# Turning the first two tiles centred, v's weights on ScalarE's queue, and a new order list

## The chip, the cores and the metric

The kernel runs on one core of one Trainium2 chip. The metric is the device time of one execution in microseconds (us). Of the kernel before there are three timed runs, and one more execution that was profiled. The core has a matrix engine (TensorE, PE in the profile, its weight loads PEld), a vector engine (VectorE, DVE), an activation engine (ScalarE, ACT), GpSimd (POOL), and SyncE (SP), which here issues transfers only. Transfers go out from the queues of SP, ACT and POOL and share 16 DMA engines.

## The reference

The input x is 2048 rows of 512, in bfloat16, and every row is normalised first (mean and variance over the 512). Two branches start from that normalised row, xn:

```python
xn = layernorm(x)
q, k, v = split(xn @ wqkv)              # 32 heads of 16
s = local_attention(q, k, v) @ wo       # row i sees rows i, i-2, ..., i-14
h = gelu(layernorm(xn) @ w1)
hs = shift_rows_by_group(h) @ w2        # four column groups, rows -1, +1, -2, +2
x1 = xn + hs
b = x1 + gelu(layernorm(x1) @ w3) @ w4  # w3 is 512x1376, w4 is 1376x512
out = x + s * silu(b)                   # the outer x, not xn
```

`layernorm` has eps 1e-5 and no learned factor. What matters here is that a row's normalisation is a subtraction of its mean and a multiplication by one number per row, so the number can also be applied after a product.

## The kernel before

The 2048 rows are 16 tiles of 128 rows, four tiles to a chunk of 512, four chunks. Tile i of chunk c holds every fourth row of the chunk. One long string, `ORDER`, lists some 700 steps such as `v.0.1` (the v product of tile 0 into PSUM bank 1), and the program issues them in just that order. Each engine runs its own steps in the order in which they stand in the list, and waits by semaphores for what it needs. A transfer also waits until the transfer that held its semaphore lane eight transfers earlier has landed. So moving a step in the list moves it past everything else on its engine or queue.

The steps around the change, with the lines of the profile:

- Loading. `ldxp.s.0` loads tiles 0 and 1 as one transfer of 256 KB from SP's queue (L221), `ldv.s.0` and `ldv.s.1` v's weights in halves of 256 KB (L234), then `ldxp.s.1` tiles 2 and 3, `ldw1.s.0` and `.1` w1 in halves (L241), two more pairs of x, and the weights of q and of k (`ldqk`, L228), 512 KB each. All go out from SP.
- Warming. `c_warm` fills a tile (L275) and `warmup` runs products on it that nobody reads (L321), ten of 512 columns before the first real work and eight of 128 columns inside it.
- Statistics. `st.i` takes a tile's mean and variance on DVE (L333 and L334). For tiles 0 to 3, `sq0.i` is the square root on ACT (L338), and `nm0.i` the reciprocal (L344) and the normalised tile `xr[i]` (L345) on DVE. For the other tiles the factor comes from a power on POOL (`rs`, L386) and the tile from `nmv` on DVE (L410) or `nm` on ACT (L417).
- Turning. The products need xn with its 512 columns on the partitions. Tiles 0 to 3 are turned on PE, `tr0.i` (L356), four transposes each, and copied out of PSUM by ACT into `xnT` of chunk 0, `ev0h` in two halves for tiles 0 and 1 (L364), `ev0a` for 2 and 3 (L360). From tile 4 on a transposing DMA does it, one for a pair of tiles, `xT.k` on SP (L424).
- Products. `v.i` (L471), copied out by `ev.i` on ACT (L481) and stored to HBM by `sv.i` on POOL (L489); `w1.i` (L496), copied out with gelu by `eh.i` (L507), whose row factor `rs` and `rr` (L397) have made; `qk.c.n` (L443), eight products for a whole chunk, copied out by `eqk` (L452).
- Later. `hTr` and `x1Tr` are transposing DMAs on SP for h and for the normalised x1; `w2`, `w3`, `w4`, `wo` are the other products; `pw` (L530), `smx`, `sms`, `smn` and `vp` (L716) are the attention's work on DVE, `lg` (L543) and `ws` (L729) its sums on PE.
- The end. Tiles 12 to 14 go through `ge` (ACT, L782), `gb` (L786) and `fav` (L819) on DVE and leave by `so` (L839). Tile 15 is done in two halves, `woh` (PE, L793), `sgh` (L802) and `favh` (L807) on DVE, `soh` (L813).

Of the kernel before, what the change touches and what calls it, by code (L numbers as in the profile page):

```python
# [20 lines left out]
st.4 tr0.3.3 rs.1 v.2.1 ev0a.3 st.7 rp.2 rs.2 w1.2.4 ev.2 st.6 eh.0 v.3.3 sv.2 rp.3 rr.1 w1.3.1  # L21
nmv.4 nmv.5 ev.3 qk.0.1.5 xT.2 eh.1 sv.3 qk.0.0.3 rs.3 qk.0.3.2 eh.2 eh.3 eqk.0.1 c_elog
qk.0.4.1 qk.0.5.5 nmv.6 nmv.7 st.11 ldxc.s.3 st.10 st.8 eqk.0.3 eqk.0.5 qk.0.2.2 eqk.0.0
qk.0.6.4 eqk.0.2 st.9 eqk.0.4 qk.0.7.3 eqk.0.6 eqk.0.7 pw.0.1 rp.5 st.15 st.13 rp.4 xT.3 hTr.0
ldw2.s hTr.1 w1.4.1 v.5.4 ldwo.s.0 ev.5 w1.5.3 v.4.2 ev.4 qk.1.4.4 rs.4 sv.4 v.6.5 w1.7.2 rr.3
rr.2 eh.4 pw.0.2 kh.1 ev.6 sv.5 rs.5 nb.4 pw.0.0 st.12 eqk.1.4 eh.5 w1.6.1 qk.1.1.4 qk.1.2.3
v.7.5 hTr.2 nm.8 nm.9 w2.1.0 pw.0.3 nb.5 rp.6 eh.6 xT.4 vl.s.1.1 eh.7 st.14 rp.7 lg.0.0 rs.7
eqk.1.2 lg.0.1 ev.7 pw.0.5 w2.0.5 rs.6 eqk.1.1 nm.11 nm.10 pw.0.4 sv.7 qk.1.5.4 sv.6 xT.5
qk.1.6.3 xa.1 nb.7 qk.1.0.2 nb.6 st3s.1 eqk.1.6 hTr.3 rr.4 xa.0 ldw3.s.0 st3s.0 eqk.1.5 pw.0.6
nm.13 nm.12 nm.15 qk.1.7.0 qk.1.3.4 w2.2.5 w1.9.3 w1.8.1 eh.9 eh.8 xa.2 rr.7 hTr.4 rr.5 rq.0  # L30
w1.10.5 pw.0.7 r3.0 v.8.3 eh.10 st3s.2 nm.14 w2.3.1 nm3.0 nm3.1 eqk.1.3 w2.5.5 ev.8 qk.2.0.4
xa.3 st3s.3 eqk.1.7 eqk.1.0 xT.6 lg.0.3 rq.1 kh.2 xa.5 lg.0.2 r3.1 w2.4.2 smx.0 ldw3.s.1 sv.8
xT.7 x1Tr.0 v.10.5 qk.2.4.0 w2.6.1 eqk.2.4 nm3.3 xa.4 ex.0 w2.7.3 w1.11.2 xa.6 st3s.6 nm3.2 xa.7
qk.2.5.1 eqk.2.0 x1Tr.1 eh.11 ev.10 sv.10 rr.6 v.9.0 v.11.3 w1.13.4 eqk.2.5 ev.9 hTr.5 qk.2.7.2
w1.15.1 eqk.2.7 w1.12.0 vl.s.2.0 vl.s.0.0 ldw4.s.2 qk.2.2.2 vl.s.3.1 eh.12 pw.1.0 st3s.4 st3s.7
st3s.5 v.12.5 eqk.2.2 pw.1.3 sms.0 eh.13 v.13.0 w3.0.6.4 ev.11 hTr.6 rq.2 qk.2.1.3 pw.1.2 r3.2
sv.9 eg.0.6 eqk.2.1 ldwo.s.3 smn.0 rq.3 pw.1.1 r3.3 w3.0.1.2 qk.2.3.4 w3.0.10.3 nm3.4 eqk.2.3
tE.0 eh.15 eg.0.10 ev.13 eg.0.1 lg.1.1 lg.1.0 pw.1.7 w2.8.1 w1.14.0 w3.0.0.2 eh.14 w3.0.2.3
hTr.7 qk.2.6.0 eqk.2.6 eg.0.0 w2.10.4 nm3.6 vl.s.0.1 nm3.7 x1Tr.3 vl.s.1.0 pw.1.5 xa.8 pw.1.4
nm3.5 pw.1.6 w2.11.1 xa.10 w3.0.8.2 xa.11 qk.3.1.4 st3s.11 eg.0.8 ev.12 w2.14.1 lg.1.2 st3s.10  # L40
sv.12 lg.1.3 eqk.3.1 w2.12.4 sv.11 st3s.8 eg.0.2 smx.1 w2.9.3 ldw4.s.1 x1Tr.2 xa.9 w2.15.5 xa.14
w3.0.3.2 w3.0.9.3 xa.12 pw.2.2 qk.3.2.1 qk.3.0.4 w2.13.0 st3s.9 eqk.3.2 eqk.3.0 eg.0.3 vl.s.9.1
ldw4.s.0 rq.4 xa.15 vl.s.9.0 vl.s.3.0 ldwo.s.2 pre.s.2 qk.3.3.1 w3.0.5.2 st3s.12 qk.3.4.5 eg.0.5
pw.2.3 eqk.3.3 qk.3.5.4 st3s.14 pw.2.4 xa.13 pw.2.1 rq.5 st3s.15 v.15.1 eqk.3.5 v.14.2 ev.15
eqk.3.4 w3.1.1.0 w3.0.4.5 vp.0 st3s.13 rq.6 pw.2.0 r3.4 nm3.9 w3.0.7.1 eg.0.4 ev.14 eg.0.9
eg.0.7 ex.1 qk.3.7.4 w3.1.0.2 eg.1.0 sv.14 r3.5 nm3.10 rq.7 nm3.11 x1Tr.5 w3.1.8.1 vl.s.2.1
# [27 lines left out]
def kernel(  # L74
# [199 lines left out]
    def c_warm():  # L274
        nc.vector.memset(warm[:], 0.0)  # L275

    @step
    def c_ident():
        make_identity(nc, ident[:])
# [4 lines left out]
        nc.gpsimd.memset(mhalf[:], -0.5)  # L284

    @step
    def c_zero():
        nc.gpsimd.dma_start(out=v_dram[0:PADK, :], in_=warm[0:PADK, :])
        nc.gpsimd.memset(hT[:, :, :, 0:HALO], 0.0)
        nc.gpsimd.memset(hT[:, :, :, HALO + S // TPC :], 0.0)  # L290

# [51 lines left out]
    def nm0(i):
        nc.vector.reciprocal(out=rstd1(i), in_=ve1[:, i // 2, i % 2 : i % 2 + 1])  # L344
        nc.vector.tensor_scalar(  # L345
            out=xr[i], in0=xtile(i), scalar1=mv1[:, i, 0:1], scalar2=rstd1(i),
            op0=ALU.subtract, op1=ALU.mult,
        )
# [3 lines left out]
    @step  # L352
    def tr0(i, b):
        tr_t[i] = bank(b, (P, ND, P), BF16)
        for dt in range(ND):
            nc.tensor.transpose(tr_t[i][:, dt, :], xr[i][:, dt * P : (dt + 1) * P], ident[:])  # L356
# [5 lines left out]
    @step  # L362
    def ev0h(i, h):
        nc.scalar.activation(  # L364
            xnT_tile(0)[:, i, 2 * h : 2 * h + 2, :], tr_t[i][:, 2 * h : 2 * h + 2, :], AF.Copy
        )
# [98 lines left out]

    @step
    def v(i, b):
        c, jj = i // TPC, i % TPC
        pt = mm["v", i] = bank(b)
        for dt in range(ND):  # L470
            nc.tensor.matmul(  # L471
                pt, lhsT=xnT[c][:, jj, dt, :], rhs=wv_sb[:, dt, :],
                start=(dt == 0), stop=(dt == ND - 1),
            )

# [14 lines left out]

    @step
    def w1(i, b):
        c, jj = i // TPC, i % TPC
        pt = mm["w1", i] = bank(b)
        for dt in range(ND):
            nc.tensor.matmul(  # L496
                pt, lhsT=xnT[c][:, jj, dt, :], rhs=w1_sb[:, dt, :],
                start=(dt == 0), stop=(dt == ND - 1),
            )

# [374 lines left out]
```

## Time and profile before

| | |
|---|---|
| median of three timed runs | 190.42 us (190.27 to 190.52) |
| profiled execution | 190.75 us |
| its span, first to last instruction | 189.0 us |
| outside the span | 1.75 us |
| mean granted TensorE clock | 0.996 |
| busy in the span: PE, DVE, ACT, POOL | 182.8, 165.1, 112.8, 42.7 us |
| moved by DMA | 39.25 MB, 208 GB/s on average |

The rows of the profile give the start and the duration of instructions on each engine, merged where the same operation repeats ("x4"), with the idle time ahead of them in square brackets and what ended it. "Issue to landing" of a transfer runs from the issuing instruction's start until all of its data has arrived. A product of 512 columns is shown with a duration of 379 ns, but the next one starts 216 ns after it: four of them take 0.86 us in the chain of waits.

### The profile page before, as it was taken

The numbers are of one execution on the slowest core, as the hardware profiler recorded it, in microseconds if no ns is written. First come the engines' busy times: TensorE is split into PE (matmuls) and PEld (weight loads), VectorE is DVE, ScalarE is ACT, GpSimd is POOL, SyncE is SP. The second block draws the span as 40 slices with busy tenths as digits, with TensorE's granted clock in tenths as the row PEclk, the third lists the DMA queues.
The fourth block names the chain that finished last, engine by engine and source line by source line (L and its number), as shares of the span: only waits on it lengthen the run. The fifth ranks groups of instructions, "written<-read, shape, count | busy, mean of one in ns | idle before, by whom it ended". The sixth has DMA issues, their size and how long they took to land.

```text
span 189.0 us, 3685 instructions
## 1 busy us (share of the span) xinstructions
PE 182.8 (97%) x1430; PEld 87.0 (46%) x1430; DVE 165.1 (87%) x270; ACT 112.8 (60%) x189; POOL 42.7 (23%) x70
## 2 busy tenths in 40 slices
PE   7999999999999999999999999999999999999990
PEld 2444445445444545444444555444455444444450
DVE  2694797997999899999989998999999999989554
ACT  3578669666595636045941465969529664742780
POOL 4157156423010702010450000000050003005350
PEclk9999999999999999999999999999999999999998
DMA  5994986987969929965989929999974999796783
GB/s 164 315 352 115 199 248 141 194 238 137 233 120 286 278 64 224 222 87 190 399 162 361 274 57 134 254 401 277 189 190 95 254 335 238 210 254 106 88 106 116
DMA packets 47842, 39.25 MB, mean 208 GB/s; under 512 B 35251, under 2 KB 41889, under 8 KB 47777
## 3 DMA queue, kind: packets, MB, share of 16 engines
q1 hardware_dynamic: 45008, 35.14, 74.6%
q0 software_dynamic: 2528, 3.69, 10.9%
q8 instruction: 11, 0.18, 0.4%
q10 hardware_dynamic: 288, 0.20, 0.3%
q14 instruction: 7, 0.05, 0.1%
HBM read 26.41 MB, written 5.78 MB: 170 GB/s over the span
## 4 chain that ended last, share of the span: by engine, by line
PE 85%; DMA 4%; DVE 4%; issue 2%; POOL 2%; SPq 1%; ACT 1%; POOLq 0%
PE mm L668 20%; PE mm L685 18%; PE mm L443 15%; PE mm L611 8%; PE mm L496 7%; PE mm L471 6%; PE lg L543 4%; PE mm L768 4%; DMA xc<-in_A_x_dram 3%; PE mm L729 3%; POOL out_dram L835 2%; DMA out_dram<-xr 1%; DVE st L333 1%; DVE xr L775 1%; DVE xr L786 1%
## 5 line engine op out<-in xcount | busy, mean ns | idle before, releaser
L530 DVE TENSOR_TENSOR pw<-qT,kT 128x2048 bf16<-128x2048 bf16 x32 | 38.3, 1214 | 3.4 <-PE lg L543 2.4
L668 PE MATMUL mm<-x1T,w_sb 128*128 128x512 bf16 (+1 forms) x176 | 40.9, 379 | 0.0
L685 PE MATMUL mm<-w_sb,h 128*128 128x512 bf16 (+1 forms) x176 | 39.4, 379 | 0.0
L677 ACT ACTIVATE h<-mm 128x512 bf16<-128x512 f32 (+1 forms) x44 | 23.9, 602 | 23.3 <-PE mm L668 17.6
L716 DVE TENSOR_TENSOR vs<-vs,att 128x4096 bf16<-128x4096 bf16 x16 | 36.2, 2285 | 0.0
L443 PE MATMUL mm<-xnT,wqk_sb 128*128 128x512 bf16 x128 | 30.6, 379 | 0.0
L835 POOL DMA_DIRECT2D out_dram<-xr x12 | 11.0, 1117 | 74.0 <-DVE xr L775 74.0
L668 PEld LDWEIGHTS <-w_sb 128*128 128x128 bf16 (+1 forms) x176 | 17.6, 100 | 20.4
L685 PEld LDWEIGHTS <-h 128*128 128x128 bf16 (+1 forms) x176 | 16.9, 98 | 20.8 <-issue 0.4
L443 PEld LDWEIGHTS <-wqk_sb 128*128 128x128 bf16 x128 | 12.4, 98 | 15.0
L452 ACT ACTIVATE kT<-mm 128x512 bf16<-128x512 f32 x16 | 9.4, 601 | 12.1 <-PE mm L443 11.9
L489 POOL DMA_DIRECT2D v_dram<-vt x16 | 9.6, 601 | 30.6 <-ACT vt L481 27.2
L471 PE MATMUL mm<-w2v_sb,xnT 128*128 128x512 bf16 x64 | 15.8, 379 | 0.0
L496 PE MATMUL mm<-w_sb,xnT 128*128 128x512 bf16 x64 | 15.8, 379 | 0.0
L611 PE MATMUL mm<-w2v_sb,hT 128*128 128x512 bf16 x64 | 15.7, 380 | 0.0
L768 PE MATMUL mm<-wo_sb,oT 128*128 128x512 bf16 x60 | 14.3, 379 | 0.0
L333 DVE BATCH_NORM_STATS2 st<-xc 128x6 f32<-128x512 bf16 x16 | 10.8, 676 | 3.9 <-DMA xc<-in_A_x_dram 3.9
L452 ACT ACTIVATE qT<-mm 128x512 bf16<-128x512 f32 x16 | 9.4, 605 | 7.8 <-PE mm L443 7.7
L635 POOL TENSOR_TENSOR rstd<-nmr,mhalf 128x2 f32<-128x2 f32 x8 | 9.1, 1136 | 19.8 <-DVE nmr L628 19.7
L507 ACT ACTIVATE ht<-mm,rs 128x512 bf16<-128x512 f32 x16 | 10.6, 690 | 4.4 <-PE mm L496 2.3
L696 ACT ACTIVATE xr<-xr 128x512 bf16<-128x512 bf16 x16 | 9.6, 630 | 6.0 <-DVE xr L692 6.0
L692 DVE TENSOR_TENSOR xr<-mm,xr 128x512 bf16<-128x512 f32 x16 | 10.6, 683 | 1.1 <-PE mm L685 0.9
(79 smaller groups left out, 218.5 us busy)
## 6 DMA issues: line engine op xcount, KB each, us to landing
vs<-v_dram SPq DMA_DIRECT2D x32, 512.0 KB, 5.8
v_dram<-vt POOLq DMA_DIRECT2D x16, 128.0 KB, 3.8
out_dram<-in_A_x_dram SPq DMA_DIRECT2D x3, 512.0 KB, 6.5
out_dram<-xr POOLq DMA_DIRECT2D x12, 128.0 KB, 3.5
w_sb<-in_B_w_dram SPq DMA_DIRECT2D x2, 688.0 KB, 4.9
w_sb<-in_B_w_dram SPq DMA_DIRECT2D x2, 640.0 KB, 6.8
xc<-in_A_x_dram SPq DMA_DIRECT2D x4, 256.0 KB, 5.9
wqk_sb<-in_A_wqkv_dram SPq DMA_DIRECT2D x2, 512.0 KB, 7.8
```

The costliest lines, as they stand in the source:

```text
L443: nc.tensor.matmul(pt, lhsT=wqk_sb[:, dt, nt * P : (nt + 1) * P], rhs=xnT[c][:, :, dt, :], start=(dt == 0), stop=(dt == ND - 1),)
L452: nc.scalar.activation(dst.rearrange("p (n i) -> p n i", i=TPC), mm.pop(("qk", c, nt)).rearrange("p (i n) -> p n i", i=TPC), AF.Copy,)
L471: nc.tensor.matmul(pt, lhsT=xnT[c][:, jj, dt, :], rhs=wv_sb[:, dt, :], start=(dt == 0), stop=(dt == ND - 1),)
L496: nc.tensor.matmul(pt, lhsT=xnT[c][:, jj, dt, :], rhs=w1_sb[:, dt, :], start=(dt == 0), stop=(dt == ND - 1),)
L530: nc.vector.tensor_tensor(out=pw_t[c, u], in0=q_t[c], in1=k_t[c][:, :, DIL * u : DIL * u + CH], op=ALU.mult)
L611: nc.tensor.matmul(pt, lhsT=hT[:, plane, g, p0 : p0 + P], rhs=w2_sb[:, g, :], start=(g == 0), stop=(g == ND - 1),)
L668: nc.tensor.matmul(pt[:fs, :], lhsT=w3_sb[:, dt, ft * P : ft * P + fs], rhs=x1T[c][:, :, dt, :], start=(dt == 0), stop=(dt == ND - 1),)
L677: nc.scalar.activation(h3[c, ft][:fs, :], mm.pop(("w3", c, ft))[:fs, :], AF.Gelu_apprx_tanh)
L685: nc.tensor.matmul(pt, lhsT=h3[c, ft][:fs, jj * P : (jj + 1) * P], rhs=w4_sb[:fs, ft, :], start=(ft == 0), stop=(ft == NF - 1),)
L716: nc.vector.tensor_tensor(out=vv, in0=vv, in1=att[c][:, :, H * jj : H * jj + H].unsqueeze(2).to_broadcast([P, NB * 2, DH, H]), op=ALU.mult,)
L768: nc.tensor.matmul(pt, lhsT=oT[i // 2][:, i % 2, dt, :], rhs=wo_sb[:, dt, :], start=(dt == 0), stop=(dt == ND - 1),)
L835: nc.gpsimd.dma_start(out=rows(out2, i), in_=xr[i], accum_op=ALU.add)
```

## The change

Seven things change.

1. Tiles 0 and 1 are no longer normalised before they are turned. A new step `cn.i` only subtracts the mean, into `cen_t`; `tr0.0` and `tr0.1` turn that; `ev0h` copies it into a tile of its own, `cenT`; and `v.0`, `v.1`, `w1.0`, `w1.1` read `cenT` (through `turned(i)`). The row factor is applied where the products leave PSUM: `ev.0` and `ev.1` scale by `rstd1`, `eh.0` and `eh.1` by the power alone, so `rr.0` goes. `rc.i` is the reciprocal, now a step by itself.
2. Tiles 0 and 1 are normalised all the same, for the residual and for q and k: `nmv.0`, `nmv.1` on DVE, and a transposing DMA `xT.0` on SP, which fills tiles 0 and 1 of `xnT` of chunk 0.
3. The first pair of x is loaded as two transfers of 128 KB (`ldx.s.0`, `ldx.s.1`), with the second pair right behind them on SP, and then w1.
4. v's weights are issued from ACT's queue (`ldv.a.0`, `ldv.a.1`). `c_warm` now also writes one element of their tile on DVE, so the first of them waits for that write, and ACT's table load and all its other work stand behind the two issues.
5. `warmup.10.512` becomes `warmup.8.512`, `warmup.8.128` becomes `warmup.5.128`.
6. `c_zero` (14 rows of zeros to HBM, from POOL's queue) moves from the head to behind `sv.2`; its two memsets are a step of their own, `c_halo`; `kh.0` moves behind `sv.3`; `c_elog` moves to the head.
7. The whole list is another one. On SP, `xT.0` stands ahead of the load of k's weights (`ldqk.s.1`) and of the next chunk's x. The head of the list, and the end:

```diff
-ldxp.s.0 c_warm c_small warmup.10.512.0 sqw c_ident kh.0 ldv.s.0 ldv.s.1 ldxp.s.1 ldw1.s.0
-ldw1.s.1 c_zero st.0 ldxp.s.2 ldxp.s.3 st.1 sq0.0 ldqk.s.0 ldqk.s.1 nm0.0 sq0.1 rp.0 nm0.1
-tr0.0.0 warmup.8.128.1 ev0h.0.0 ev0h.0.1 st.2 tr0.1.2 v.0.1 st.3 ev0h.1.0 ev0h.1.1 sq0.2 v.1.2
-ev.0 nm0.2 sq0.3 rp.1 w1.0.0 ev.1 nm0.3 rs.0 sv.0 st.5 tr0.2.1 ldxc.s.2 w1.1.2 ev0a.2 sv.1 rr.0
+ldx.s.0 c_warm c_small c_ident c_elog ldx.s.1 ldv.a.0 warmup.8.512.0 ldxp.s.1 ldv.a.1 sqw st.0
+cn.0 st.1 tr0.0.1 ev0h.0.0 ev0h.0.1 sq0.0 sq0.1 ldw1.s.0 ldw1.s.1 ldxp.s.2 ldqk.s.0 ldxp.s.3
+warmup.5.128.0 cn.1 st.2 tr0.1.0 v.0.1 ev0h.1.0 st.3 sq0.2 ev0h.1.1 v.1.2 rc.0 rp.1 rc.1 ev.0
+nm0.2 w1.1.0 sq0.3 nmv.1 rp.0 sv.0 nmv.0 tr0.2.1 rs.0 nm0.3 w1.0.3 xT.0 ev0a.2 st.4 ev.1 rs.1
+tr0.3.4 v.2.1 st.5 rp.2 ev0a.3 ldqk.s.1 eh.1 ldxc.s.2 w1.2.2 st.7 rs.2 w1.3.4 st.6 sv.1 ev.2
+v.3.5 rp.3 nmv.4 rs.3 qk.0.3.1 nmv.5 ev.3 rr.1 xT.2 c_sel qk.0.2.0 qk.0.0.5 nmv.6 eqk.0.3 nmv.7
...
-woh.15.1.2 soa.10 sg.11 soa.11 ge.13 gb.13 ge.14 fav.13 gb.14 so.s.13 ge.12 fav.14 gb.12 so.s.14
-sgh.15.0 fav.12 favh.15.0 so.a.12 sgh.15.1 soh.s.15.0 favh.15.1 soh.a.15.1
+soa.8 eoT.14 eoT.15 eoT.13 wo.14.3 eoT.12 wo.13.4 ge.14 wo.12.1 gb.14 ge.13 fav.14 si.12
+woh.15.0.3 gb.13 so.s.14 ge.12 woh.15.1.4 fav.13 sgh.15.0 so.s.13 sgh.15.1 gb.12 favh.15.1
+favh.15.0 soh.a.15.1 fav.12 soh.s.15.0 so.a.12
```

The steps themselves:

```diff
     def c_warm():
         nc.vector.memset(warm[:], 0.0)
+        nc.vector.memset(wv_sb[0:1, 0, 0:1], 0.0)
...
+    def turned(i):
+        return cenT[:, i, :, :] if i < 2 else xnT[i // TPC][:, i % TPC, :, :]
+    def cn(i):
+        nc.vector.tensor_scalar(out=cen_t[:, i, :], in0=xtile(i),
+            scalar1=mv1[:, i, 0:1], scalar2=None, op0=ALU.subtract)
+    def rc(i):
+        nc.vector.reciprocal(out=rstd1(i), in_=ve1[:, i // 2, i % 2 : i % 2 + 1])
...
-            nc.tensor.transpose(tr_t[i][:, dt, :], xr[i][:, dt * P : (dt + 1) * P], ident[:])
+            src = cen_t[:, i, :] if i < 2 else xr[i]
+            nc.tensor.transpose(tr_t[i][:, dt, :], src[:, dt * P : (dt + 1) * P], ident[:])
...
-            xnT_tile(0)[:, i, 2 * h : 2 * h + 2, :], tr_t[i][:, 2 * h : 2 * h + 2, :], AF.Copy
+            cenT[:, i, 2 * h : 2 * h + 2, :], tr_t[i][:, 2 * h : 2 * h + 2, :], AF.Copy
...
     def ev(i):
             AF.Copy,
+            scale=rstd1(i) if i < 2 else 1.0,
...
-                pt, lhsT=xnT[c][:, jj, dt, :], rhs=w1_sb[:, dt, :],
+                pt, lhsT=turned(i)[:, dt, :], rhs=w1_sb[:, dt, :],
```

More of the change, by code (lines that the diff above doesn't have):

```diff
@@ L23 @@
[L23 to L46, printed above, removed]
@@ L208, in ldxc, with ldx @@
     @step
+    def ldx(q, i):
+        if 0 not in x_c:
+            x_c[0] = rot("xc", 0, 2, [P, TPC, D])
+        qs[q].dma_start(out=xtile(i), in_=rows(x2, i))
+    @step
     def ldxc(q, c):
@@ L286, in c_zero, with c_halo @@
     @step
-    def c_zero():
-        nc.gpsimd.dma_start(out=v_dram[0:PADK, :], in_=warm[0:PADK, :])
+    def c_zero(q):
+        qs[q].dma_start(out=v_dram[0:PADK, :], in_=warm[0:PADK, :])
+    @step
+    def c_halo():
         nc.gpsimd.memset(hT[:, :, :, 0:HALO], 0.0)
@@ L340, in sq0 @@
         )
+    cen_t = sb.tile([P, 2, D], BF16, name="cen", tag="pw0")
+    cenT = sb.tile([P, 2, ND, P], BF16, name="cenT", tag="pw1")
+    def turned(i):
+        return cenT[:, i, :, :] if i < 2 else xnT[i // TPC][:, i % TPC, :, :]
+    @step
+    def cn(i):
+        nc.vector.tensor_scalar(
+            out=cen_t[:, i, :], in0=xtile(i), scalar1=mv1[:, i, 0:1], scalar2=None,
+            op0=ALU.subtract,
+        )
+    @step
+    def rc(i):
+        nc.vector.reciprocal(out=rstd1(i), in_=ve1[:, i // 2, i % 2 : i % 2 + 1])
     @step
@@ L471, in v @@
             nc.tensor.matmul(
-                pt, lhsT=xnT[c][:, jj, dt, :], rhs=wv_sb[:, dt, :],
+                pt, lhsT=turned(i)[:, dt, :], rhs=wv_sb[:, dt, :],
                 start=(dt == 0), stop=(dt == ND - 1),
@@ L831, in pre, with preh @@
         )
+    @step
+    def preh(q):
+        i = NT - TPC
+        qs[q].dma_start(out=rows(out2, i), in_=rows(x2, i))
     @step
```

73 lines of the change are left out of this document (45 added, 28 removed).

## The prediction

> **What bounds the kernel now.** I read the page's busy shares first, then the windows by stage.
>
> ```profile
> PE 182.8 (97%) x1430; PEld 87.0 (46%) x1430; DVE 165.1 (87%) x270; ACT 112.8 (60%) x189; POOL 42.7 (23%) x70
> ```
>
> ```profile
> 3.00:5.00 2.00, 2.00 (x7) 0.63 (x5) 1.35 (x3) 0.30 (x1) 0.00 (x0) 1.00 0.83 268
> 5.00:7.00 2.00, 1.76 (x17) 1.13 (x16) 1.30 (x7) 0.78 (x3) 0.71 (x1) 1.00 0.79 246
> 7.00:10.00 3.00, 2.86 (x16) 1.13 (x13) 2.04 (x7) 2.03 (x7) 0.11 (x1) 1.00 1.05 377
> 10.00:170.05 160.05, 159.92 (x1287) 76.31 (x1288) 147.89 (x234) 99.35 (x162) 32.74 (x49) 1.00 0.89 217
> ```
>
> After the stretch's length come the busy times of PE, PEld, DVE, ACT and POOL, the granted clock, the share of the DMA engines and GB/s. From 10 us on PE is idle for 0.13 of 160 us. The number of products does not change, so in this stretch a new list can only lose. What can be won lies ahead of 10 us, and behind the last product. The timeline of the head:
>
> ```profile
> 0.73 0.40 SPq L221 DMA_DIRECT2D xc<-in_A_x_dram  x1
> 1.18 4.45 PE L321 MATMUL mm<-warm 128*128 128x512 bf16 x10 [1.18 <-DVE warm L275]
> 3.61 0.69 DVE L333 BATCH_NORM_STATS2 st<-xc 128x6 f32<-128x512 bf16 x1 [2.49 <-DMA xc<-in_A_x_dram]
> 4.34 0.18 DVE L334 BATCH_NORM_AGGREGATE mv<-st 128x2 f32<-128x6 f32 x1
> 5.24 0.13 DVE L344 RECIPROCAL rs<-ve 128x1 f32<-128x1 f32 x1
> 5.41 0.41 DVE L345 TENSOR_SCALAR xr<-xc,mv,rs 128x512 bf16<-128x512 bf16 x1
> 5.87 0.61 PE L356 MATMUL mm<-ident,xr 128*128 128x128 bf16 x4 [0.24 <-DVE xr L345]
> 6.27 0.72 PE L321 MATMUL mm<-warm 128*128 128x128 bf16 x8
> 6.52 1.40 ACT L364 ACTIVATE xnT<-mm 128x256 bf16<-128x256 bf16 x4 [0.86 <-PE mm L356]
> 7.06 1.94 PE L471 MATMUL mm<-w2v_sb,xnT 128*128 128x512 bf16 x8
> 7.85 0.70 DVE L333 BATCH_NORM_STATS2 st<-xc 128x6 f32<-128x512 bf16 x1 [1.44 <-DMA xc<-in_A_x_dram]
> 8.80 0.30 ACT L338 ACTIVATE ve<-mv,eps_t 128x1 f32<-128x1 f32 x1 [0.88 <-DVE mv L334]
> 8.83 1.03 PE L496 MATMUL mm<-w_sb,xnT 128*128 128x512 bf16 x4
> 9.64 0.41 DVE L345 TENSOR_SCALAR xr<-xc,mv,rs 128x512 bf16<-128x512 bf16 x1
> 10.11 0.40 PE L356 MATMUL mm<-ident,xr 128*128 128x128 bf16 x4 [0.26 <-DVE xr L345]
> 14.96 7.07 PE L443 MATMUL mm<-xnT,wqk_sb 128*128 128x512 bf16 x32
> 15.17 1.32 SPq L424 DMA_TRANSPOSE xnT<-xr  x1
> ```
>
> The first useful product starts at 7.06. Two waits are to be seen. x lands at 3.6, and statistics, root, reciprocal, normalising, turning and copying take the 3.45 us from there. And PE stands still once more before 10.11, for tile 2. The chain of waits says why:
>
> ```profile
> 2.15 5.68 DMA xc<-in_A_x_dram
> ...
> 15.13 6.91 PE mm L443 x32
> ```
>
> The second pair of x, issued at 2.15, lands at 7.83, and all up to 10.11 follows from it. A product of 512 columns costs 6.91/32 = 0.216 us, a step of four 0.86. The views by source give landings from issue (least, median, most):
>
> ```profile
> L234 SPq DMA_DIRECT2D w2v_sb<-in_A_wqkv_dram x2: 414/442/470, 1.2 to 1.6; - x2
> DMA to landing us min/median/max: 3.1/4.3/5.5
> ...
> L241 SPq DMA_DIRECT2D w_sb<-in_B_w_dram x2: 434/452/469, 2.7 to 3.1; - x2
> DMA to landing us min/median/max: 5.8/5.9/6.0
> ...
> L424 SPq DMA_TRANSPOSE xnT<-xr x6: 1231/1250/2395, 15.2 to 45.5; - x6
> DMA to landing us min/median/max: 3.1/4.2/7.1
> ```
>
> So v's second half is there at 1.64 + 5.5 = 7.1, and w1's halves at about 8.5 and 9.2, while the first w1 product, 8.83, reads the second half from 8.83 + 0.43 = 9.26 on. The loads come just in time: a shorter chain to 7.06 is worth nothing unless they come earlier too.
>
> **The change, part by part.**
>
> *x in two transfers.* The first 128 KB at the 268 GB/s of the row take half of what 256 KB took, about 0.5 us less. Bounds: nothing, to 0.5 us. I take 0.4: tile 0 is there at 3.2.
>
> *Centred.* From landing to the end of the mean is 4.52 − 3.61 = 0.91 us; `cn.0` has the form of L345, 0.41. It ends at 4.55 where L345 ended at 5.82: root and reciprocal leave the path. The eight warm-ups end at 1.18 + 8 × 0.427 = 4.6 and cover it. `tr0.0` starts at 4.6, and the copies end at about 5.95, by the distance from 5.87 to 6.52 and 0.35 a copy. `st.1` and `cn.1` follow on DVE until 5.95, `tr0.1` lasts until 6.2, and `v.0` can start at 6.25 instead of 7.06: 0.8 us. The scalings ride on copies that are there anyway. `nmv.0`, `nmv.1`, `cn` and `rc` against `nm0` and `rr` are about 0.7 us more of DVE, and DVE waited 1.44 us for x at 7.85. Without that cover they would cost the 0.7.
>
> *The loads.* Ahead of the end of w1 stand the same 1,536 KB as before. The rate decides. In the rows 3 to 7 us DVE and PE needed data and the DMA engines were at 0.83 and 0.79, with 268 and 246 GB/s; afterwards 377. Had the 1.03 MB of these 4 us gone at 377 GB/s, they would have taken 2.7 us: all later landings 1.3 us earlier. That is one bound, no gain is the other. I take the faster one, because half of the issues now leave from a second queue and the zeros (`c_zero`, POOL) no longer go out among them; neither is shown by a row, so the chance below stays near half. x's second pair then has 768 to 1,024 KB at or ahead of it, depending on how v's 512 KB interleave: before, these amounts were in at 7.1 and 7.8, less 1.3 is 5.8 to 6.5. I take 6.2. v's second half is there by 6.5, w1's by 7.9.
>
> *The new waits on ACT.* The first issue of v's weights waits for two writes on DVE; behind it stand the second, the table load and everything else of ACT, all done before 5.2, when its first copy is due. That costs nothing. But `sq0.2` now stands ahead of `ev0h.1.1`, and it needs the second pair of x. So `v.1` gets its second half of columns at 6.2 + 0.91 + 0.30 + 0.35 + 0.1 of handovers = 7.85; without this wait it would be at 7.56 (6.25 + 0.86 + 0.43 + a little). It ends at 8.3, `w1.1` at 9.15. Tile 2 is normalised, from the landing, after 10.05 − 7.83 = 2.2 us plus the two reciprocals put ahead of it, 0.3: at 8.7, in time. `tr0.2` starts at 9.15 instead of 10.11. `nm0.3` is queued behind `nmv.1`, `rp.0` and `nmv.0` (L410's price is below) and ends at 10.3, PE needs it at 10.23: 0.1 lost. The q products then come 0.85 us earlier than 14.96, at 14.1.
>
> ```profile
> L410 DVE TENSOR_SCALAR xr<-xc,mv,rs 128x512 bf16<-128x512 bf16 x4 | 1.6, 442 | 2.5 <-POOL rs L386 2.4
> ```
>
> *The transposing DMA.* q and k of chunk 0 now need `xT.0`. `nmv.0` ends at 8.7 + 2 × 0.44 + 0.16 = 9.75. Landing 3.1, 4.2 or 7.1 us later is 12.9, 14.0 or 16.9; needed at 14.1. At the median it is just covered by the eight products of v and w1. Behind it on SP wait k's weights and the next x: issued at about 11.1 instead of 5.15, k's weights are first read after three q products, 2.6 us into that stage, at 16.7; I price that at nothing, at most 0.5.
>
> *Warm-ups, `c_halo`, `c_elog`, `kh.0`.* POOL and PE do these while they wait; nothing.
>
> *The rest of the list.* I compared, in PE work, how far each transposing DMA stands ahead of its first reader. The least is 4 products in the list before and 7 in the new one for `xT` to a q or k product, 5 and 7 for `hTr` to `w2`, 9 and 11 for `x1Tr` to `w3`. That is no closer than before, where PE did not wait. Gain impossible, price from 0 to 1; I take 0.
>
> *The end.*
>
> ```profile
> 183.51 1.04 PE L793 MATMUL mm<-wo_sb,oT 128*128 128x256 bf16 x8
> 185.47 0.37 ACTq L839 DMA_DIRECT2D out_dram<-xr  x1
> 186.00 0.29 DVE L807 TENSOR_TENSOR xr<-xc,xr 128x256 bf16<-128x256 bf16 x1
> 186.37 0.34 ACTq L813 DMA_DIRECT2D out_dram<-xr  x1
> ...
> out_dram<-xr ACTq DMA_DIRECT2D x1, 128.0 KB, 1.9
> out_dram<-xr ACTq DMA_DIRECT2D x1, 64.0 KB, 1.6
> ```
>
> The same DVE steps follow the last product, in another order; the last transfer is now tile 12's 128 KB, 1.9 us instead of 1.6, and `ge.12` stands behind a silu. DVE starts tile 15 sooner. From −0.1 to 0.5; I take 0.2.
>
> The sum: −0.85 + 0.2 = −0.65. The profiled execution would go from 190.75 to 190.1, with a span of 188.35; it lay 0.33 above the median, so the median goes from 190.42 to 189.8.
>
> **The rivals.**
>
> *The loads share one road.* If the rate of 3 to 7 us stays, x's second pair lands at 7.1 to 7.8, v's second half, now interleaved with x, at 7.8 instead of 7.1. Then `v.0` stops in its middle from 6.7 to 7.8 and ends at 8.25; `v.1` waits behind `sq0.2` for 7.5 + 1.65 = 9.15 and ends at 9.6; `tr0.2` comes at 10.45, 0.35 later than before, between 0 and 0.7. With the end: 190.4 to 191.3, likely 190.95. It decides from a landing of x's second pair at about 7.2 on. For it: the DMA engines were at 0.8 busy already. Against it: 377 GB/s is possible. The Trainium skill, "DMA: Bandwidth & Descriptors", section "Issuing engines are not separate DMA queues", says that transfers issued from several engines run on the same 16 engines and interleave, and that only the issuing time is saved. By that rule this rival holds, and ACT's queue helps nothing; the trace of before has one queue at work there and can't show it.
>
> *`xT.0` comes late.* It lands 7.1 us after its issue as the slowest did: PE waits 16.9 − 14.1 = 2.8 us, 192.6; one at 5.6 gives 191.1. It decides from 4.9 us on, where the 0.65 are used up. For it: k's weights, x's chunk and v's stores are on the same engines then. Against it: the one issued at 15.17 met little traffic, as this one will if the loads are early.
>
> *The new list stalls later.* DVE has 147.9 of 160 us in the long stretch; a wait of PE for `pw` or `vp` gives back 0.3 to 1.2 us: 190.1 to 191.
>
> *A cold clock.* The granted clock reads 1.00 in all rows above, but the warm-ups cost 0.427 each, twice 0.216; the transition falls into the row at 6.27, where eight products of 128 columns take 0.72. With fewer warm-ups and more gaps it may come later: up to eight products at twice the price, 1.7 us, less what waits anyway. The Trainium skill, "TensorE: Matmul & The Clock Gate", Part 1, has the full rate after about 3.4 us of sustained work in a free-running window, which gives the same time in both lists or one window later.
>
> **How the numbers follow.** A measurement of this kernel can tell about 0.2% (0.38 us) from no change: 190.04 to 190.80. The forecast 45%, with 189.3 to 190.1 as its own range; shared loads 25%; late `xT.0` 12%; later stalls 13%; cold clock 5%. Of the forecast some 3% falls within 0.2%, of the four rivals together some 12%, and some 3% of them still end faster. So faster 0.45, same 0.15, slower 0.40. The range from 189.3 to 191.4 leaves out the fastest loads with no loss at the end, and the latest `xT.0`.
>
> **What would show it.** Right: the second statistics wait of DVE ends before 6.6; the first v product starts at about 6.3, with no gap inside it; `tr0.2` before 9.4; the q products by 14.2; PE idle under 0.3 us from there on; the last transfer lands about 3.7 us after the last product's start. Wrong: a gap inside the first eight v products, which is the shared road; a gap ahead of the first q product, which is `xT.0`; any PE wait for DVE after 25 us, which is the list.

## The result

The changed kernel takes 189.24 us (median of 7 runs, 189.17 to 189.72); the kernel before took 190.27 (median of 7, 189.83 to 190.52). The ratio is 0.9965, with a 95% interval from 0.9954 to 0.9977: about 0.66 us faster. The medians differ by more, 1.03, but three of the seven times of before (190.27, 190.42, 190.52) are the three known ahead of the prediction; the four others are 189.83, 189.84, 189.88 and 190.30, and 189.24 lies 0.62 below their median of 189.86. One execution of e3 below took 494.76 us and one of e4 389.99; no figure here includes them. The profiled execution took 189.17 with a span of 187.4, against 190.75 and 189.0 before.

The busy shares in the page of the changed kernel, and its windows by stage (columns as before):

```profile
PE 180.3 (96%) x1410; PEld 86.2 (46%) x1425; DVE 165.6 (88%) x272; ACT 114.7 (61%) x190; POOL 41.8 (22%) x70
```

```profile
3.00:5.00 2.00, 1.94 (x13) 0.78 (x12) 1.73 (x4) 0.70 (x3) 0.69 (x4) 1.00 0.88 304
5.00:7.00 2.00, 1.41 (x13) 0.68 (x10) 1.82 (x6) 1.62 (x7) 0.00 (x0) 1.00 1.09 377
7.00:10.00 3.00, 3.00 (x20) 1.52 (x19) 2.89 (x13) 2.03 (x6) 1.29 (x2) 1.00 1.01 343
10.00:170.05 160.05, 159.20 (x1273) 76.11 (x1284) 147.61 (x231) 101.96 (x164) 30.32 (x46) 1.00 0.87 216
```

The second row shows the largest difference between the two profiles: between 5 and 7 us the DMA engines moved 377 GB/s, where they had moved 246. In the last row PE seems idle for 0.85 us, but PEld counts 1284 weight loads there and PE 1273 products: some product records are missing. The timeline below has a measure that needs no count. The head:

```profile
1.19 0.98 ACTq L241 DMA_DIRECT2D w2v_sb<-in_A_wqkv_dram  x2
...
3.20 0.69 DVE L345 BATCH_NORM_STATS2 st<-xc 128x6 f32<-128x512 bf16 x1 [2.06 <-DMA xc<-in_A_x_dram]
...
4.14 0.35 DVE L363 TENSOR_SCALAR cen<-xc,mv 128x512 bf16<-128x512 bf16 x1
...
4.55 0.40 PE L387 MATMUL mm<-ident,cen 128*128 128x128 bf16 x4
...
4.79 0.44 PE L333 MATMUL mm<-warm 128*128 128x128 bf16 x5
...
5.82 0.40 PE L387 MATMUL mm<-ident,cen 128*128 128x128 bf16 x4 [0.59 <-DVE cen L363]
...
5.83 0.69 DVE L345 BATCH_NORM_STATS2 st<-xc 128x6 f32<-128x512 bf16 x1
...
6.05 2.00 PE L501 MATMUL mm<-w2v_sb,cenT 128*128 128x512 bf16 x8
...
7.89 1.03 PE L526 MATMUL mm<-w_sb,cenT 128*128 128x512 bf16 x4
...
8.75 0.39 PE L387 MATMUL mm<-ident,xr 128*128 128x128 bf16 x4
...
9.06 1.39 SPq L455 DMA_TRANSPOSE xnT<-xr  x1
...
13.52 7.07 PE L474 MATMUL mm<-xnT,wqk_sb 128*128 128x512 bf16 x32
```

Tile 0 is there at 3.20 (before 3.61). `v.0` starts at 6.05 (before 7.06), tile 2 is turned at 8.75 (before 10.11), q and k start at 13.52 (before 14.96). The statistics of tile 2 start at 5.83 and wait for nothing: x's second pair landed at 5.81, where it had landed at 7.83. The tail:

```profile
182.05 1.04 PE L823 MATMUL mm<-wo_sb,oT 128*128 128x256 bf16 x8
...
184.22 0.42 DVE L849 TENSOR_TENSOR xr<-xc,xr 128x512 bf16<-128x512 bf16 x1
184.37 0.33 SPq L843 DMA_DIRECT2D out_dram<-xr  x1
184.67 0.36 ACTq L871 DMA_DIRECT2D out_dram<-xr  x1
```

From the first q product to the last product step it is 182.05 − 13.52 = 168.53 us. Before it was 183.51 − 14.96 = 168.55. So the new order of these 168 us is worth nothing in either direction. From the last step to the end of the span it is 187.4 − 182.05 = 5.35, before 189.0 − 183.51 = 5.49. The profiled pair differs by 1.58: 1.44 at the head, 0.02 in the long stretch and 0.14 at the end, less 0.02 by which the time outside the span grew.

But the runs differ by 0.66, not 1.58. The profiled execution of before was a late one: the spans of its 27 runs of the first set below lie between 188.0 and 188.7, with a median of 188.1, and its profile had 189.0. (In a later set of 29 runs, beside h1, e3 again and g1, they go from 188.0 to 189.5, with a median of 188.5.) Late loads, 7.83 and 7.17 for x's second pair and v's second half, are what its trace shows; e1 below, with the same loads at its head, had them 0.70 and 1.02 earlier and started q and k 0.69 earlier. The median spans of that first set and of the changed kernel, 188.1 and 187.5, differ by 0.6. By estimate, then, a typical run gains about 0.5 at the head and 0.14 at the end.

### The profile page after: what moved, and what is told of

Its sections match the earlier page's. It is cut to its first block, busy times and chain, and to the rows that moved or that the text cites. A ratio compares the mean times of both kernels' runs of the same rounds, so it can differ in the third digit from the quotient of the medians.

```text
span 187.4 us, 3672 instructions
## 1 busy us (share of the span) xinstructions
PE 180.3 (96%) x1410; PEld 86.2 (46%) x1425; DVE 165.6 (88%) x272; ACT 114.7 (61%) x190; POOL 41.8 (22%) x70
## 3 DMA queue, kind: packets, MB, share of 16 engines
q0 software_dynamic: 2528, 3.69, 9.9%
## 4 chain that ended last, share of the span: by engine, by line
PE 92%; DVE 3%; DMA 1%; issue 1%; ACT 1%; DVEq 0%
PE mm L698 20%; PE mm L715 20%; PE mm L474 15%; PE mm L526 7%; PE mm L501 7%; PE mm L641 7%; PE mm L798 6%; PE lg L573 4%; PE mm L759 4%; DMA xc<-in_A_x_dram 1%; DVE st L345 1%; DVE xr L816 1%; DVE xr L849 1%; PE mm L387 0%; ACT oT L792 0%
## 5 line engine op out<-in xcount | busy, mean ns | idle before, releaser
L698 PE MATMUL mm<-x1T,w_sb 128*128 128x512 bf16 (+1 forms) x176 | 40.1, 379 | 0.0
L501 PE MATMUL mm<-w2v_sb,xnT 128*128 128x512 bf16 x54 | 14.0, 380 | 0.1
L526 PE MATMUL mm<-w_sb,xnT 128*128 128x512 bf16 x54 | 13.8, 380 | 0.2
```

Source lines behind the costliest of these rows:

```text
L501: nc.tensor.matmul(pt, lhsT=turned(i)[:, dt, :], rhs=wv_sb[:, dt, :], start=(dt == 0), stop=(dt == ND - 1),)
L526: nc.tensor.matmul(pt, lhsT=turned(i)[:, dt, :], rhs=w1_sb[:, dt, :], start=(dt == 0), stop=(dt == ND - 1),)
L698: nc.tensor.matmul(pt[:fs, :], lhsT=w3_sb[:, dt, ft * P : ft * P + fs], rhs=x1T[c][:, :, dt, :], start=(dt == 0), stop=(dt == ND - 1),)
```

## The experiments

Milestones of all profiles, in us. "time" is that of the profiled execution, "q/k" the start of the first q and k products, "rest" the distance from there to the last product step; GB/s is of the window from 5 to 7 us. Each row is one execution. The changed kernel was timed in the one set above; the experiments ran in other sets, each with before beside it, and are compared with the changed kernel by their ratios to before or by spans.

| kernel | time | GB/s | v.0 | tile 2 turned | q/k | rest |
|---|---|---|---|---|---|---|
| before | 190.75 | 246 | 7.06 | 10.11 | 14.96 | 168.55 |
| e1 zeros late | 190.06 | 245 | 6.88 | 9.51 | 14.27 | 168.55 |
| e3 loads only | 189.57 | 382 | 6.43 | 9.06 | 13.83 | 168.55 |
| e3 again | 189.73 | 378 | 6.55 | 9.19 | 13.95 | 168.56 |
| h1 v on ACT only | 190.21 | 346 | 6.64 | 9.65 | 14.42 | 168.54 |
| e4 centred only | 191.32 | 321 | 6.23 | 9.08 | 14.94 | 169.21 |
| after | 189.17 | 377 | 6.05 | 8.75 | 13.52 | 168.53 |
| e2 zeros early | 189.74 | 369 | 6.04 | 9.36 | 14.12 | 168.54 |
| e5 v on SP | 191.07 | 257 | 6.18 | 9.66 | 15.08 | 168.53 |
| e6 no short wait | 189.97 | 374 | 6.54 | 9.23 | 13.99 | 168.54 |
| e7 w1 first | 191.12 | 384 | 5.99 | 10.72 | 15.48 | 168.54 |
| e8 not centred | 190.11 | 376 | 6.87 | 9.46 | 14.22 | 168.53 |
| g1 halves | 191.22 | 381 | 5.63 | 9.15 | 14.66 | 169.47 |
| g2 halves, mended | 190.28 | 383 | 5.58 | 8.71 | 13.47 | 169.72 |

In 11 of the 14 the rest is 168.53 to 168.56. Whatever a change of the head brings or costs at q/k arrives at the end in full.

**Zeros late, and zeros early.** Before, with its store of zeros moved behind the second halo:

```diff
-ldw1.s.1 c_zero st.0 ...        rr.2 eh.4 pw.0.2 kh.1 ev.6
+ldw1.s.1 c_halo st.0 ...        rr.2 eh.4 pw.0.2 kh.1 c_zero ev.6
```

> The kernel before, with nothing changed but the store of 14 rows of zeros: it leaves POOL's queue behind the second chunk's halo instead of at the head. Theory A (the zeros, in flight from about 1.5 to 5.5 us beside the first loads, hold one or two DMA engines up and make the last pieces of x's second pair and of v's weights late): the second pair lands about 1 us earlier than 7.83, tile 2 is turned at about 9.5 instead of 10.11, faster by 0.3 to 0.5 us. Theory B (the order and the queues of the loads made the difference, or the centring): same within 0.15 us.

Measured: 189.91 against 189.92, ratio 1.000 (0.999 to 1.001). Theory A falls for this kernel. Its profile has the same loads at the head as that of before. The last pieces of v's second half and of x's second pair come at 6.15 and 7.13 instead of 7.17 and 7.83, and the time is 0.69 us less, though the medians are equal: this is a difference from run to run, called the draw below.

After, with the zeros back at the head:

```diff
-ldx.s.0 c_warm c_small c_ident c_elog ldx.s.1
+ldx.s.0 c_warm c_small c_ident c_zero.g c_elog ldx.s.1
...
-kh.1 c_zero.g rs.5
+kh.1 rs.5
```

> The changed kernel, with nothing put back but the zeros on POOL's queue at the head. Theory A (the zeros hold the loads up): the second pair of x and v's second half land up to 1.3 us later than 5.81 and 6.55, slower than the changed kernel by 0.3 to 0.7 us, that is 189.5 to 189.9. Theory B (they don't): 189.24 within 0.15 us.

Measured: 189.57 (189.13 to 190.00), ratio to before 0.9976 (0.9964 to 0.9988), which overlaps with the 0.9965 of the changed kernel. Its profile shows v's second half at 7.00 and a wait of 0.41 us for it. A cost of 0.2 (by the ratios) to 0.3 (by the median spans, 187.8 and 187.5) is possible and not settled.

**The loads alone.** Before's list and normalised tiles, with the new loads:

```diff
-ldxp.s.0 c_warm c_small warmup... kh.0 ldv.s.0 ldv.s.1 ldxp.s.1 ldw1.s.0
+ldx.s.0 c_warm c_small ldx.s.1 ldv.a.0 ldxp.s.1 ldv.a.1 warmup... kh.0 ldw1.s.0
```

> The kernel before, its list and its normalised tiles, with the changed kernel's loads alone: x's first pair in two transfers, the second pair right behind them, v's weights on ACT's queue behind the one-element write, then w1. Theory L (most of the gain is the second pair's landing, which sets tile 2): the pair lands at about 5.8 to 6.2, tile 2 is turned at about 9.5 instead of 10.11, faster by 0.3 to 0.6 us. Theory C (most of it is the centring, which starts the first product 1 us earlier): faster by 0.2 us at most.

> The kernel before with the changed kernel's loads alone, once more, for a second profile: its times lay in two groups, 189.5 to 189.7 as in its profile and 189.9 to 190.6. If the upper group comes from late pieces of a load, this profile, should it fall in that group, shows tile 2 turned after 9.4 and the time again at 180.5 us behind that; if it comes from the list behind 10 us, tile 2 is turned at 9.06 again and PE waits later.

Measured: 190.00, ratio 0.9999 (0.9986 to 1.0013), and in the second set 189.81, ratio 0.9976 (0.9956 to 0.9996). Together the loads alone bring 0 to 0.4 us. The two profiles show what they would bring with good landings: the pair at 5.56 and 6.24, tile 2 turned at 9.06 and 9.19.

```profile
6.43 1.93 PE L477 MATMUL mm<-w2v_sb,xnT 128*128 128x512 bf16 x8
...
8.20 1.03 PE L502 MATMUL mm<-w_sb,xnT 128*128 128x512 bf16 x4
...
9.06 0.39 PE L362 MATMUL mm<-ident,xr 128*128 128x128 bf16 x4
```

This is the timeline of the first: from 6.43 on PE has no gap until tile 2 is turned; three steps of 0.86 us make the 2.6. Here the first product sets the pace, and it waits for the normalising. Neither profile is of one of its longer runs (up to 190.6), so what lengthens those was not seen.

**The centring alone.** Before's list and loads, with `cn`, `rc`, `nmv.0`, `nmv.1` and `xT.0` in the places that they have in the changed kernel as far as the old list lets them.

```diff
-st.0 ldxp.s.2 ldxp.s.3 st.1 sq0.0 ldqk.s.0 ldqk.s.1 nm0.0 sq0.1 rp.0 nm0.1 tr0.0.0
+st.0 cn.0 ldxp.s.2 ldxp.s.3 st.1 ldqk.s.0 ldqk.s.1 cn.1 tr0.0.0
-rs.0 sv.0 st.5 tr0.2.1 ldxc.s.2
+rp.0 nmv.0 nmv.1 rs.0 sv.0 st.5 tr0.2.1 xT.0 ldxc.s.2
```

> The kernel before, its list and its loads, with the centring of tiles 0 and 1 alone (turned centred, row factors at the copies out of PSUM, the transposing DMA for tiles 0 and 1 added). Theory L (the landings of v's second half at 7.17 and of x's second pair at 7.83 hold what follows): the first v product starts earlier, at about 6.3, and stops inside its eight until 7.2; tile 2 is turned no earlier than 10.1; time between 0.1 faster and 0.3 slower. Theory C: the first product's 0.8 to 1.0 us come through, faster by 0.5 us or more.

Measured: 191.15 (five runs), ratio 1.0056 (1.0036 to 1.0075), 1.1 us slower, more than either theory gave. The landings were good in this profile (5.41 and 6.38), so Theory L's wait is not what it shows. Its waits of PE:

```profile
PE mm L712 <- DMA w_sb<-in_B_w_dram: 0.5, 1, 0.5
PE mm L471 <- DMA xnT<-xr: 0.5, 1, 0.5
PE mm L523 <- ACT vt L508: 0.3, 1, 0.3
```

Tile 2 is turned at 9.08, 0.43 earlier than in the profile of e1, which has before's list and the same queue. Then `xT.0`, issued at 10.51, lands at 14.90, and the q products wait for it until 14.94. So the prediction's second rival, a late `xT.0`, is real; the new list issues it at 9.06. The third row is `w1.1`, which waits for the copy of the first v step. The first row lies at 93 us: a load of `w_sb`, issued from SP, comes late; that the transfer added on SP is the reason was not tried.

**v's weights back on SP.** After, with one queue:

```diff
-ldx.s.1 ldv.a.0 warmup.8.512.0 ldxp.s.1 ldv.a.1
+ldx.s.1 ldv.s.0 warmup.8.512.0 ldxp.s.1 ldv.s.1
-        nc.vector.memset(wv_sb[0:1, 0, 0:1], 0.0)
```

> The changed kernel with v's weights issued from SP's queue, at the same places of the order, and without the one-element write. Theory Q (a second issuing queue raises the rate of the first loads): x's second pair and v's second half land 0.5 to 1.3 us later than 5.81 and 6.55, slower by 0.4 to 1.0 us. Theory R (one road: the queue that issues saves issue time alone, and all five issues are out before the first lands): landings as in the changed kernel within 0.3 us, time 189.24 within 0.2.

Measured: 190.49, ratio to before 1.0028 (1.0016 to 1.0041), 1.25 us slower than the changed kernel; 0.9 of it lies in the span (medians 188.4 and 187.5). That is what Theory Q said.

```profile
5.00:7.00 2.00, 1.94 (x14) 1.21 (x12) 1.85 (x6) 1.60 (x7) 0.00 (x0) 1.00 0.94 257
```

```profile
7.47 1.46 PE L497 MATMUL mm<-w2v_sb,cenT 128*128 128x512 bf16 x6 [0.32 <-DMA w2v_sb<-in_A_wqkv_dram]
...
8.97 1.33 SPq L451 DMA_TRANSPOSE xnT<-xr  x1
...
9.66 0.39 PE L383 MATMUL mm<-ident,xr 128*128 128x128 bf16 x4
...
15.08 1.24 PE L470 MATMUL mm<-xnT,wqk_sb 128*128 128x512 bf16 x5 [0.50 <-DMA xnT<-xr]
```

The pair of x is early (5.73), but the last piece of v's second half comes at 7.43 and that of w1 at 9.18, each 1.7 to 2.0 behind the first of the 16 engines' pieces; the first pieces are no later than in the changed kernel (5.72 against 5.77, 7.22 against 7.33). So it is not the later issue. `v.0` stops in its middle, as the prediction's first rival has it, and the landing of `xT.0`, 6.0 us behind its issue, brings its second rival as well.

**Without the short wait.** The one-element write is taken out, so v's first half is issued at 0.74 beside x.

```diff
-        nc.vector.memset(wv_sb[0:1, 0, 0:1], 0.0)
```

> The changed kernel without the one-element write that ACT's first issue waits for, so that v's weights go out beside x's first tile instead of 0.45 us behind it. If the short wait matters: x's first tile shares the engines and lands at about 3.6 instead of 3.17, all of the head moves by that, slower by 0.3 to 0.4 us. If not (x's packets go first anyway, or v's earlier landing pays for it): same within 0.15 us.

Measured: 189.91, ratio 0.9997 (0.9989 to 1.0006). Tile 0 lands at 3.69 instead of 3.17, q and k start 0.47 later, the median span is 187.8 against 187.5. That is the 0.3 to 0.4 expected; another 0.35 lies outside the span (last section).

**w1 ahead of x's second pair.**

```diff
-warmup.8.512.0 ldxp.s.1 ldv.a.1 sqw ... ldw1.s.0 ldw1.s.1
+warmup.8.512.0 ldv.a.1 ldw1.s.0 ldw1.s.1 ldxp.s.1 sqw ...
```

> The changed kernel with w1 issued ahead of x's second pair, as the kernel before had neither. The pair then lands at about 8.0 instead of 5.8. If the order of the loads is what the gain of the head hangs on: v's second product step waits behind the square root of tile 2 until about 9.5, tile 2 is turned at 10.4 to 10.9, q and k start at 15.2 to 15.7 instead of 13.5, 190.9 to 191.4. If tile 2 is hidden behind the products: 189.24 within 0.3.

Measured: 191.31, ratio 1.0072 (1.0059 to 1.0084). At 384 GB/s, no less than the changed kernel's 377, the order alone costs 2.1 us:

```profile
7.84 0.69 DVE L343 BATCH_NORM_STATS2 st<-xc 128x6 f32<-128x512 bf16 x1 [2.14 <-DMA xc<-in_A_x_dram]
...
9.41 0.61 PE L499 MATMUL mm<-w2v_sb,cenT 128*128 128x512 bf16 x2 [1.90 <-ACT cenT L393]
```

The second row is the new wait on ACT that the prediction priced: the copy of tile 1's second half stands behind the root of tile 2, and the product comes 1.57 us after tile 2's statistics start (the prediction reckoned 1.65 from the landing).

**Not centred.** After's loads and list, tiles 0 and 1 normalised as before.

```diff
-st.0 cn.0 st.1 tr0.0.1 ev0h.0.0 ev0h.0.1 sq0.0 sq0.1 ... warmup.5.128.0 cn.1
+st.0 sq0.0 st.1 sq0.1 nm0.0 tr0.0.1 ev0h.0.0 ev0h.0.1 ... warmup.5.128.0 nm0.1
```

> The changed kernel, its loads and its list, with tiles 0 and 1 normalised before they are turned, as before (root and reciprocal back on the way to the first product; no transposing DMA for them, no second normalising, no row factors at the copies). If the centring brings something beside the loads: the first v product starts at 6.4 to 6.9 instead of 6.05, q and k at 13.9 to 14.3 instead of 13.52, slower by 0.3 to 0.8 us. If the loads set the pace anyway: same within 0.15 us.

Measured: 190.18, ratio 1.0024 (1.0002 to 1.0046); two of its eleven runs, at 191.84 and 191.89, lie 1.3 us above the next. The median span is 188.2, 0.7 more than after. `v.0` starts at 6.87, 0.82 later than after.

```profile
5.45 0.61 PE L385 MATMUL mm<-ident,xr 128*128 128x128 bf16 x4 [0.66 <-DVE xr L373]
5.85 0.74 PE L331 MATMUL mm<-warm 128*128 128x128 bf16 x5
...
6.87 1.89 PE L499 MATMUL mm<-w2v_sb,xnT 128*128 128x512 bf16 x8
...
14.22 1.89 PE L472 MATMUL mm<-xnT,wqk_sb 128*128 128x512 bf16 x8
```

Not all of the 0.82 is the centring. The same four transposes and five warm-ups take 5.85 + 0.74 − 5.45 = 1.14 us here and 4.79 + 0.44 − 4.55 = 0.68 in the changed kernel: here they start 0.107 us apart, there 0.056. Tile 1's transposes wait for the last of them, so by estimate 0.46 of the 0.82 is this lower rate of PE and about 0.4 the centring. Whether the other runs of e8 had it too can't be seen.

**The queue alone on the kernel before.**

```diff
-ldxp.s.0 c_warm c_small warmup.10.512.0 sqw c_ident kh.0 ldv.s.0 ldv.s.1 ldxp.s.1
+ldxp.s.0 c_warm c_small ldv.a.0 ldv.a.1 warmup.10.512.0 sqw c_ident kh.0 ldxp.s.1
```

> The kernel before with one thing changed: v's weights are issued from ACT's queue behind the one-element write, everything else as it was. Theory Q (a second issuing queue lets the DMA engines move the first loads at 370 to 385 GB/s between 5 and 7 us, where one queue gave 245 to 320): the window from 5 to 7 us shows over 360 GB/s, the last of the 16 engines is less than 1 us behind the first in every load, x's second pair lands by 6.6, tile 2 is turned at 9.4 to 9.5; faster than the median of before by up to 0.3 us, since before often has that luck anyway. Theory R (the queue does not matter; the changed kernel's loads are faster for another reason, such as their order or the split of x): 245 to 320 GB/s as in the other kernels with one queue, same time within 0.15.

Measured: 190.64, ratio 1.0023 (1.0006 to 1.0041): slower. The rate did rise, to 346 GB/s, but the pieces were not all within 1 us (1.1 to 1.9), and the order turned against the kernel: x's second pair, now issued at 1.18, landed at 5.00, and v's halves at 6.22 and 7.46, behind it and half of w1. Theory Q is half right: in this profile the rate is higher, but the time goes with the order of what lands.

**A step further, twice.** The first v step in two halves, the first ahead of the turning of tile 1, and v's second half, now from SP's queue, ahead of x's second pair:

```diff
-ldv.a.0 warmup.8.512.0 ldxp.s.1 ldv.a.1 ... cn.1 st.2 tr0.1.0 v.0.1 ev0h.1.0 st.3 sq0.2 ev0h.1.1 v.1.2
+ldv.a.0 warmup.8.512.0 ldv.s.1 ldxp.s.1 ... vh.0.0.3 cn.1 sq0.1 tr0.1.0 vh.0.1.3 ev0h.1.0 ev0h.1.1 v.1.2
```

> A further step from the changed kernel, at the limits its trace shows (the first v product waits for tile 1 to be turned, its third for v's second half at 6.55): the first v step is cut in two halves, the first ahead of the turning of tile 1; v's second half is issued ahead of x's second pair; tile 2's statistics and normalising come ahead of tile 3's; the root of tile 2 stands behind both copies of tile 1. If PE's own chain sets tile 2: first v product at 5.4 instead of 6.05, tile 2 turned at 8.45 to 8.6 instead of 8.75, q and k at about 13.25, faster than the changed kernel by 0.15 to 0.3 us. If tile 2's landing, now behind v's second half (about 6.5), sets it: tile 2 turned at 8.8 to 9.1, same or slower by up to 0.4.

> The halved v step and the earlier v weights of the attempt before, with the two waits mended that its trace shows behind the head: the third v copy now stands ahead of the first Gelu (whose table load it waited behind, 0.6 us ahead of the first q product), and the second normalising of tile 1 ahead of tile 3's statistics, so that the transposing DMA goes out earlier. If those waits were all that it lost: no wait of PE between 10 and 30 us, q and k at 13.3 to 13.9 by the draw of the loads, 188.9 to 189.5, that is the changed kernel's time or up to 0.3 us less. If tile 2 and tile 3, now late by v's weights ahead of their x, push the copies and the transposing DMAs anyway: 189.6 to 190.2.

Measured: 190.18, ratio 0.9992 (0.9972 to 1.0011), and 190.38, ratio 1.0018 (0.9999 to 1.0038). In the second profile q and k start at 13.47, a little ahead of the changed kernel, and the new waits behind the head went. But PE then stands still once more:

```profile
PE mm L473 <- DMA xnT<-xr: 1.0, 1, 1.0
```

```profile
25.02 1.02 PE L473 MATMUL mm<-xnT,wqk_sb 128*128 128x512 bf16 x4 [1.02 <-DMA xnT<-xr]
```

This is chunk 1's second transposing DMA, issued at 16.91 (after: 15.94) and landed at 24.97 (after: 21.52). With tile 3 pushed back on DVE, all its later steps come 1 us later; the rest is the transfer's own time, 8.06 us from issue to landing instead of 5.58, and why it took that long is not shown. Neither version beats the changed kernel.

## Why the prediction came out as it did

The forecast was 189.8 and faster, from −0.85 at the head and +0.2 at the end; measured are 189.24 and, in the profiles, −1.44 and −0.14. As a time, 189.24 lies 0.06 below the stated range of 189.3 to 191.4; the measured ratio on the prediction's base of 190.42 would be 189.75, next to the forecast. Step by step:

- *What bounds the kernel.* Right: PE without a gap from 10 us on, and the head its only reserve. The column "rest" shows it: 168.53 to 168.56 us in 11 kernels.
- *x in two transfers.* Predicted 3.2, measured 3.20. The short wait on ACT is part of it: without it, e6, tile 0 lands 0.5 later.
- *Centred.* `tr0.0` at 4.6 predicted, 4.55 measured; `v.0` at 6.25 predicted, 6.05 measured. Its price was taken from the old rows as 0.8. e8 gives back 0.82 at `v.0`, but with 0.46 of that put down to PE's lower rate, about 0.4 is left by estimate. The two profiles of e3, normalised and at the full rate from their first transposes on, start `v.0` at 6.43 and 6.55, 0.4 to 0.5 behind the changed kernel, with three more short warm-ups (about 0.17) ahead of it. So at an equal rate of PE the price was likely set too high.
- *The loads.* The faster bound was taken for two reasons of which it was said that "neither is shown by a row". The first, the second queue, holds (e5: 257 instead of 377 GB/s); the second, the zeros, had no effect on the old kernel (e1) and an unsettled one on the new (e2). x's second pair came at 5.81 instead of 6.2, at the near end of the 5.8 to 6.5 given; v's second half at 6.55 (6.5 predicted), w1's at 8.02 (7.9).
- *The new wait on ACT* was over-priced: 0.29 predicted, nothing measured. With the pair at 5.81 the root was done at 7.07 and the copy at 7.34, and `v.1` needed it at 7.46. e7 shows that the wait is real when the pair is late. In its place v's second half cost 0.11 inside `v.0`, which the prediction had listed as a sign of the shared road.
- *The transposing DMA.* Issued at 9.06 instead of 9.75, landed 3.35 us later instead of 4.2, at 12.41: covered by 1.1 us. e4 and e5 show it uncovered.
- *The head in sum* is the term that was mis-sized most: −0.85 against −1.44. Of the 0.59, 0.2 is `v.0`'s earlier start, 0.29 the wait on ACT that did not come, 0.1 the wait for `nm0.3` that did not come, less 0.11 for v's second half; these make 0.48. The other 0.1 is a stop that the prediction carried over unseen: in before, PE waits 0.08 behind tile 2's last transpose (10.29, next product 10.43), within the 4.85 from there to q and k; in the changed kernel that stretch takes 4.77.
- *The rest of the list.* 0, as taken.
- *The end* had the wrong sign: +0.2 predicted, −0.14 measured, though within the bounds. The smaller last transfer was given up, but DVE starts and finishes its last additions earlier relative to the last step: the last issue leaves 184.67 − 182.05 = 2.62 behind it, before 186.37 − 183.51 = 2.86. The larger transfer takes 1.79 to land instead of 1.57, so the last landing comes 4.41 behind the last step instead of 4.43. Most of the 0.14 thus lies behind the last landing, and its reason is open.
- *The profile against the median.* The prediction took the profiled execution of before as 0.33 above the median of three runs. Over the 27 runs of the first set it lay 0.83 above (189.92). So the base of the sum was half a microsecond too high, which is nearly all of the 0.56 between 189.8 and 189.24. The measured gain of 0.66 is next to the predicted 0.65 by luck: the late draw of before, in the sum, stood against the terms that were priced too low, and against a typical run the head brings about 0.5 and not 0.85.
- *The rivals.* Both landing rivals exist and were each called up by one edit: the shared road in e5, `xT.0` late in e4 and e5. The cold clock did not cost the changed kernel anything, though the granted clock of 1.00 can't show it: it reads 1.00 over warm-ups 0.427 us apart too. The starts show it: transposes 0.056 apart from 4.62 on, where in before they were 0.107 apart until about 6.5. So the full rate came some 2 us earlier than in before, not at the same time or later as the prediction had it. The Trainium skill, "DMA: Bandwidth & Descriptors", section "Issuing engines are not separate DMA queues", has only issue time to be saved by a second issuing engine; here the trace disagrees for the window from 5 to 7 us: 245, 246, 257 and 321 GB/s in the four profiles with one queue for the loads, 346 to 384 in the ten with two (g1 and g2 with v's first half alone on the second). The orders differ among these, and each is one execution; the pairs that differ in little else have 246 and 346 (before and h1), 257 and 377 (e5 and the changed kernel).

What no single part explains is the combination. Loads alone: 0 to 0.4 faster. Centring alone: 1.1 slower. Loads and list without the centring: 0.45 slower (its interval barely leaves out no change), 0.2 of it outside the span. All but the second queue: 0.5 slower, 0.3 of it outside the span. All together: 0.66 faster. Three chains of nearly the same length meet ahead of tile 2, from x's first tile, from v's weights and from x's second pair, and a fourth, `xT.0`, ahead of q and k; shortening one shows the next.

## What to carry to other kernels

Where PE is full behind a short head, measure a change by when the first step of the full stretch starts: the distance from there to the last product step differs by at most 0.03 us among 11 of these 14 profiles. Several near-equal chains meet in such a head, so undoing one part of a change can cost more than the whole brings, and a part tried alone can look harmful; try the parts by taking them out of the whole too. And take a single profile's late landings for a draw: before it is used as the base of a sum, see how its time lies among a dozen runs. Before two heads are compared, see by the distance between PE's starts whether both ran at the full rate.

## What the runs showed of the hardware

- With all first loads on SP's queue, the last of the 16 engines' pieces came up to 2.5 us behind the first (before); with v's weights on ACT's queue, 0.3 to 2.0, mostly under 1. The split is not clean: e4, with one queue, has 0.55 to 0.93, and e2, h1 and g1, with two, mostly over 1. In the traces, packets of 1 and 2 KB mostly take 0.05 and 0.08 us, but some take 0.4 to 0.9: 21 of them between 2 and 9 us in the four profiles with one queue (2 to 10 each), 0 to 3 in each of the ten with two. Why a second queue goes with fewer of them was not found.
- PE's products start at half the rate at first: 0.427 us apart for 512 columns and 0.107 for 128, later 0.216 and 0.056. The change came by 4.6 us in the changed kernel, at about 6.5 in before and between 6.3 and 6.6 in e8; in the two profiles of the same kernel e3 at 4.5 and not before 5.0. The granted clock reads 1.00 in the window from 3 to 5 us of before, where all products are at half the rate. What it costs hangs on what waits anyway: nothing in before's profile, where tile 2 waited for x, about half a microsecond in that of e8.
- The time outside the span depends on the kernel: 1.75 to 1.8 us in most, but 2.1 to 2.15 in e5 and e6 and 2.0 in e8, the same in every run of a kernel to 0.1. It made e6 cost 0.67 instead of the 0.35 that its span shows. What it hangs on stays open; differences of a few tenths should be compared by spans as well.
